# Five routing groups instead of six, a floor inside a scan, and a reordered passage between attention and mixture of experts

## The chip, the cores and the metric

The kernel runs on one core of a Trainium2 chip. Its time is device microseconds from launch to end; the median of three runs before the change is 373.67 us (373.53 to 373.78). The profile is of a separate execution, recorded by the hardware profiler. Engines are called PE (TensorE, matrix products; PEld is its weight load), DVE (VectorE), ACT (ScalarE), POOL (GpSimd) and SP (SyncE, which here only issues transfers). Each engine works through its own queue in order and waits on semaphores for the others.

## The reference

Attention with a decaying state, then a top-1 mixture of experts on its output, all in float32:

```python
for t in range(S):                       # B, H, S, D = 4, 8, 768, 48
    state = alpha[:, :, t, :, None] * state + einsum('bhd,bhe->bhde', k[:, :, t], v[:, :, t])
    y[:, :, t] = einsum('bhd,bhde->bhe', q[:, :, t], state)
x = y.transpose(0, 2, 1, 3).reshape(3072, 384)
logits = x @ w_gate + modality_bias[modality_id]       # 8 experts, 2 modalities
e_idx = argmax(logits); gate_w = softmax(logits)[e_idx]
for e in range(8):
    mask = e_idx == e
    out[mask] = gate_w[mask, None] * (relu(x[mask] @ w1[e]) @ w2[e])   # 384 -> 1024 -> 384
```

## The kernel before, in words

**Attention.** The 3072 tokens are 24 chunks of 128 tokens, one chunk per step, some 5.5 us each. In a step DVE makes the decay products of the chunk with two scans: `decay` scans backwards to G (L254), `decay_back` takes the column `amin` out of G with a floor (L262), its reciprocal (L263), and scans forwards to Fw (L265). G times the transposed keys is kh (L281), Fw times the transposed queries is qh (L289). PE transposes kh back (L295), multiplies qh with the state (L327) and with kh (L307), and after a causal select on POOL (L312) multiplies the scores with the values (L334). The state update is POOL's (L356, L358). The rows of the result, y, are transposed again (L365), multiplied with the gate weights (L377), and the products are turned into logits (L385, L387).

**Routing.** When the logits of a group of chunks are there, `route_flow` adds the bias table, finds the winning expert and each token's rank among that expert's tokens (L445 to L473: six DVE operations to `oh`, products with a triangle and with ones on PE, then ranks and the one-hot table `OL`). `GROUPS` says which chunks form a group and after which step it starts. Flows are generators: every step takes each of them one `yield` further, so the work of a flow is spread over steps. Two experts are begun early (`EARLY`): at the given chunk `route_early` picks an expert that already has 256 tokens, finds their places (products at L567), and `gather` fetches their rows (xg, POOL's indirect transfers, L689). After the second early expert `gates_flow` computes the gates of all tokens so far (gt, L673 to L675), PE transposes them (L678), ACT copies them (gs, L680), SP writes them to memory (gd, L685), and `gather_gates` fetches the early experts' gates (gg, POOL, L695).

**The passage.** Behind the last attention step stands a hand-written sequence in which `first_unit(0)` to `first_unit(7)` fill PE: each is three float32 products of the first layer of the first early expert (L124). Between them stand the last group, the count of each expert's tokens and the plan of slots (`route_end`, L592 to L621: nj, nn, ..., diag on DVE; key and meta), the tables of places (L636 to L648), and the gather for the third slot. `relu` makes hH and hL from a unit pair (ACT L823, DVE L825).

**Mixture of experts.** Every float32 operand of a product is split in a high and a low part: ACT casts the high part (w1H, w2H, hH), the low part is the difference (w1L, w2L by `split`, L833). A layer-2 product is the three products w2H·hH, w2L·hH and w2H·hL (L1001 to L1003). Four splits `split2(0, 0)` to `split2(0, 3)` prepare w2 of the first early expert; each serves two of the eight blocks of 128 hidden units.

**What sets the order.** On PE, DVE and ACT the order is the order of the code. The order on POOL and SP is set by a scheduler, so POOL's operations, its gathers among them, stand in one queue whose sequence the code alone doesn't show. Weights are loaded by SP in halves of 768 KB (w1r L661, w2r L663).

Of the kernel before, what the change touches and what calls it, by code (L numbers as in the profile page):

```python
# [8 lines left out]
F32 = mybir.dt.float32  # L9
# [5 lines left out]
ALU = mybir.AluOpType  # L15
# [6 lines left out]
P = 128  # L22
# [3 lines left out]
SEG = P + 1  # L26
# [15 lines left out]
U = T // P  # L42
NG = 2 * E

EARLY = (16, 18)
NA = len(EARLY)
NE = NA * TE // T
SU = N // T
# [7 lines left out]
AMIN = 1.0e-17  # L56
AFLOOR = 1.0e-30

GROUPS = ((5, 0, 6), (11, 6, 12), (15, 12, 16), (17, 16, 18), (21, 18, 22), (23, 22, 24))


@with_exitstack
def attention_moe(ctx: ExitStack, tc: tile.TileContext, q, k, v, alpha, mid, wg, mb, w1, w2, out):
# [13 lines left out]
    na = nctx.enter_context(tc.tile_pool(name="na", bufs=1, side="right"))  # L77
# [78 lines left out]
                wg.rearrange("(h c g d) e -> c g d h e", c=2, g=2, d=D)[c, g],  # L156
            )
    DR = na.tile([P, SEGS], F32, name="DR")[:, : NP * SEG + 1]
    vec.memset(DR, 0.0)
    vec.memset(DR[:, SEG :: SEG], 1.0)  # L160
    X, DF, T1 = [], [], []
    for i in range(2):
# [49 lines left out]
    def bias_table():  # L212
        mf = ac.tile([NU, P], F32, name="mf")
        vec.tensor_copy(mf, mi[:, :, 0])
        yield
        mp = ps.tile([P, NU], F32, name="sc", bufs=2)
        pe.transpose(mp, mf, ident[:NU, :NU])
        mt = ac.tile([P, NU], F32, name="mt")
        vec.tensor_copy(mt, mp)
        tmp = ac.tile([P, NU, E], F32, name="btt")  # L220
        for m in range(NM):
            sel = ac.tile([P, NU], F32, name=f"msel{m}")
            vec.tensor_scalar(sel, mt, float(m), None, op0=ALU.is_equal)
            vec.tensor_tensor(
                tmp if m else bt,
                sel.unsqueeze(2).broadcast_to([P, NU, E]),
                mbb[:, m].unsqueeze(1).broadcast_to([P, NU, E]),
                op=ALU.mult,
            )
            if m:  # L230
                vec.tensor_tensor(bt, bt, tmp, op=ALU.add)
# [19 lines left out]
    def decay(i):  # L251
        x = X[i % 2]
        G = na.tile([P, SEGS], F32, name="G", bufs=4)[:, : NP * SEG + 1]
        vec.tensor_tensor_scan(  # L254
            G[:, 1:][:, ::-1], x[:, 1:][:, ::-1], DR[:, 1:][:, ::-1], 0.0, op0=ALU.mult, op1=ALU.add
        )
        st[i, "G"] = G

    def decay_back(i):
        x, d, G = X[i % 2], DF[i % 2], st[i, "G"]  # L260
        ac1 = amin[:, i]
        vec.tensor_scalar(ac1, G[:, 1::SEG], AFLOOR, None, op0=ALU.max)  # L262
        vec.reciprocal(d[:, 0::SEG], ac1)  # L263
        Fw = na.tile([P, SEGS], F32, name="Fw", bufs=3)[:, : NP * SEG]
        vec.tensor_tensor_scan(Fw, x[:, :-1], d, 0.0, op0=ALU.mult, op1=ALU.add)  # L265
        st[i, "F"] = Fw
# [167 lines left out]
    def route_flow(t0, t1):  # L434
        n = t1 - t0
        s = slice(t0, t1)
        sh = [P, n, E]

        def wide(a, m=E):
            return a[:, s].unsqueeze(2).broadcast_to([P, n, m])  # L440

        def over(a, m=E):
            return a.unsqueeze(1).broadcast_to([P, n, m])

        vec.tensor_tensor(L[:, s], L[:, s], bt[:, s], op=ALU.add)  # L445
        vec.tensor_reduce(mx[:, s], L[:, s], axis=AX.X, op=ALU.max)
        vec.tensor_tensor(ls[:, s], L[:, s], wide(mx), op=ALU.subtract)
        vec.scalar_tensor_tensor(eq[:, s], ls[:, s], 0.0, over(rev), op0=ALU.is_equal, op1=ALU.mult)
        vec.tensor_reduce(m2[:, s], eq[:, s], axis=AX.X, op=ALU.max)
        vec.tensor_tensor(oh[:, s], eq[:, s], wide(m2), op=ALU.is_equal)  # L450
        yield
        rp = ps.tile([P, n, E], F32, name="sc", bufs=2)
        pe.matmul(rp, tri, oh[:, s], start=True, stop=False)
        for t in range(t0, t1 - 1):
            m = t1 - 1 - t
            pe.matmul(
                rp[:, t + 1 - t0 :], ones, oh[:, t].unsqueeze(1).broadcast_to([P, m, E]), start=False, stop=False
            )
        pe.matmul(rp, ones, ohs.unsqueeze(1).broadcast_to(sh), start=False, stop=True)
        vec.tensor_tensor(rk[:, s], rp, oh[:, s], op=ALU.mult)  # L460
        yield
        with nc.allow_low_precision("whole numbers"):
            vec.tensor_reduce(r1[:, s], rk[:, s], axis=AX.X, op=ALU.add)
        if t1 == NU and n > 2:
            vec.tensor_reduce(hsum, oh[:, t0 : t1 - 1].rearrange("p t e -> p e t"), axis=AX.X, op=ALU.add)
            vec.tensor_tensor(ohs, ohs, hsum, op=ALU.add)
        elif t1 < NU:
            vec.tensor_reduce(hsum, oh[:, s].rearrange("p t e -> p e t"), axis=AX.X, op=ALU.add)
            vec.tensor_tensor(ohs, ohs, hsum, op=ALU.add)
        vec.tensor_scalar(hr[:, s], r1[:, s], 7, None, op0=ALU.arith_shift_right)  # L470
        vec.tensor_scalar(lo[:, s], r1[:, s], P - 1, None, op0=ALU.bitwise_and)
        vec.scalar_tensor_tensor(hi[:, s], m2[:, s], -float(NU), hr[:, s], op0=ALU.mult, op1=ALU.add)
        vec.tensor_tensor(OL[:, s], over(ioh, P), wide(lo, P), op=ALU.is_equal)  # L473
# [113 lines left out]
    def route_end(na):  # L587
# [3 lines left out]
        cnt = ps.tile([P, E], F32, name="kv")  # L591
        pe.matmul(cnt, ones, ohs, start=True, stop=False)  # L592
        pe.matmul(cnt, ones, left, start=False, stop=False)
        if na:
            pe.matmul(cnt, ones, oh[:, NU - 2], start=False, stop=False)
        pe.matmul(cnt, ones, oh[:, NU - 1], start=False, stop=True)
        vec.tensor_tensor(
            nj.rearrange("p e u j -> p e (u j)"),
            cnt.unsqueeze(2).broadcast_to([P, E, 2 * NJ]),
# [69 lines left out]
    def gates_flow(t0, t1):  # L669
        z = slice(t0, t1)  # L670
        sh = [P, t1 - t0, E]
        act.activation(ls[:, z], ls[:, z], AF.Exp)
        vec.tensor_reduce(sm[:, z], ls[:, z], axis=AX.X, op=ALU.add)  # L673
        vec.tensor_scalar(sm[:, z], sm[:, z], 1e-9, None, op0=ALU.add)
        vec.reciprocal(gt[:, z], sm[:, z])  # L675
        yield
        gp = ps.tile([t1 - t0, P], F32, name="kv")
        pe.transpose(gp, gt[:, z], ident)  # L678
        gs = cp.tile([t1 - t0, P], F32, name=f"gs{t0}_{t1}")
        act.copy(gs, gp)  # L680
        m = min(max(MID // P, t0), t1)
        yield
        for a, b in ((t0, m), (m, t1)):
            if a < b:
                sp.dma_start(gd[row(a) : row(a) + (b - a) * P].rearrange("(t p) o -> t (p o)", p=P), gs[a - t0 : b - t0])  # L685
# [98 lines left out]
    def group_flow(t0, t1):  # L784
        yield from route_flow(t0, t1)
        if t1 in EARLY:
            e = EARLY.index(t1)
            yield from route_early(e)
            gather(e, early_cols(e), row(t1))
            if e == NA - 1:  # L790
                yield from gates_flow(0, t1)
                for e in range(NA):
                    gather_gates(e, early_cols(e), row(t1))
# [3 lines left out]
    def advance():  # L797
        for f in list(flows):
            if next(f, f) is f:
                flows.remove(f)  # L800
# [24 lines left out]
        vec.scalar_tensor_tensor(hL, hp, 0.0, hH.bitcast(F32), op0=ALU.max, op1=ALU.subtract)  # L825
        return hH, hL

    def split(name, src):
        p = hpool[name]
        hi = p.tile(list(src.shape), F32R, name=name + "H", bufs=4)  # L830
        act.copy(hi, src)  # L831
        lw = p.tile(list(src.shape), F32R, name=name + "L", bufs=4)
        vec.tensor_tensor(lw, src, hi.bitcast(F32), op=ALU.subtract)  # L833
        return hi, lw

    def split1(w, j):
        return split("w1", WR[w][0][:, :, 2 * P * j : 2 * P * (j + 1)])

    def split2(w, j):
        return split("w2", WR[w][1][:, 2 * j : 2 * j + 2])  # L840

    route_begin()
    mctx = ExitStack()
# [52 lines left out]
    hpool["h"] = rctx.enter_context(tc.tile_pool(name="hp", bufs=8, side="right"))  # L896
    w2s, hs = {0: []}, {0: []}

    advance()
    early = flows.pop()  # L900
    logits(L0 - 2)
    state(L0 - 1)
    scores(L0)
    outputs(L0 - 1)
    logits_rows(L0 - 2)
    group = route_flow(GROUPS[-1][1] - 4, GROUPS[-1][1])
    next(group)
# [5 lines left out]
    for _ in group:
        pass
    next(early)
    first_inputs()
    logits(L0)
    rows(L0)
    logits_rows(L0)
    last = route_flow(GROUPS[-1][1], NU)  # L920
    next(last)
    flag = out_of_range()
    next(flag)
    first_unit(0)
    next(last)
    ends = route_end(NE)
    next(ends)
    first_unit(1)
    next(early)
    first_unit(2)  # L930
    next(ends)
    hs[0].append(relu(hp0[0], [P, 2, TE]))
    for _ in last:
        pass
    first_unit(3)
    for _ in flag:
        pass
    next(ends)
    w2s[0].append(split2(0, 0))
    first_unit(4)  # L940
    first_unit(5)
    hs[0].append(relu(hp0[1], [P, 2, TE]))
    for _ in ends:
        pass
    gather(2, slot_cols(1))
    for _ in early:
        pass
    first_unit(6)
    w2s[0].append(split2(0, 1))
    hs[0].append(relu(hp0[2], [P, 2, TE]))  # L950
    first_unit(7)
    w2s[0].append(split2(0, 2))
    hs[0].append(relu(hp0[3], [P, 2, TE]))
    w2s[0].append(split2(0, 3))

    actx.close()
    ectx = ExitStack()
# [291 lines left out]
```

## Time and profile before

| | |
|---|---|
| median of 3 runs | 373.67 us |
| profiled execution | 376.24 us, span 374.5 us, mean granted clock 0.990 |
| PE busy | 358.7 us, 96% |
| DVE busy | 225.1 us, 60% |
| ACT busy | 188.8 us, 50% |
| POOL busy | 149.2 us, 40% |
| attention steps | about 5 to 146 us of the span |
| passage | about 146 to 164 us |
| mixture of experts | about 164 us to the end |

In a timeline row stand the start, the duration, the engine, the line, the operation with output and inputs, the tile and the number of instructions; in brackets, how long the engine idled before it and what it waited for. A wait row gives the total, the number of waits and the longest. A row of stretches gives for each engine the busy time, then the granted clock of TensorE as a share of full speed, the share of the transfer engines and GB/s.

### The profile page before, as it was taken

To read this page: it belongs to the slowest core of one execution; us is meant where nothing else is said; L and a number is where in the kernel's file an instruction comes from. 1 tells how busy PE (TensorE), PEld (TensorE's weight loads), DVE (VectorE), ACT (ScalarE), POOL (GpSimd) and SP (SyncE) were. 2 spreads that over 40 slices of the span, in tenths; PEclk is the share of its full clock that TensorE was granted. 3 is DMA by queue.
4 is the path that set the end of the run, shared out by engine and by line. 5 is a ranking of instruction groups with operands and counts; after the bars stand their busy time and mean duration, and the time that the engine had idled before them with its cause. 6 is when DMAs were issued, how large, how long until landed. Compare 5 with 4: busy or idle time off the path is not lost. (4 is left out here: it accounts for less than half of the span.)

```text
span 374.5 us, 9357 instructions
## 1 busy us (share of the span) xinstructions
PE 358.7 (96%) x3663; PEld 315.8 (84%) x3663; DVE 225.1 (60%) x458; ACT 188.8 (50%) x367; POOL 149.2 (40%) x212
## 2 busy tenths in 40 slices
PE   7899899999999898999999999999999999999992
PEld 3788788888888696779998898899889988978992
DVE  6888879788989977885845506531660456036400
ACT  2677676776767564436555425433551445164410
POOL 9745336425436445163146335412722371220031
PEclk9999999999999899999999999999999999999997
DMA  9999999999999996668756326431723373110011
GB/s 136 162 168 165 197 184 198 192 182 186 191 191 188 206 333 232 220 207 316 215 168 196 126 79 224 155 107 47 270 84 123 128 223 111 69 44 5 1 45 49
DMA packets 122730, 59.18 MB, mean 158 GB/s; under 512 B 102857, under 2 KB 114168, under 8 KB 122676
## 3 DMA queue, kind: packets, MB, share of 16 engines
q1 hardware_dynamic: 118196, 48.78, 58.7%
q0 software_dynamic: 4032, 9.68, 7.7%
q8 instruction: 31, 0.51, 0.6%
q14 instruction: 23, 0.19, 0.2%
q10 hardware_dynamic: 448, 0.01, 0.1%
HBM read 49.01 MB, written 9.50 MB: 156 GB/s over the span
## 5 line engine op out<-in xcount | busy, mean ns | idle before, releaser
L967 POOL DMA_INDIRECT out_dram<-os,odx x23 | 23.4, 1016 | 110.4 <-ACT os L1035 94.7
L312 POOL TENSOR_SCALAR_AFFINE_SELECT scT<-scT 128x512 f32<-128x512 f32 x48 | 38.8, 831 | 65.8 <-ACT scT L311 65.7
L1001 PE MATMUL sc<-w2H,hH 128*128 128x384 f32 x192 | 65.0, 339 | 0.0
L1002 PE MATMUL sc<-w2L,hH 128*128 128x384 f32 x192 | 64.5, 336 | 0.5 <-DVE w2L L833 0.3
L1003 PE MATMUL sc<-w2H,hL 128*128 128x384 f32 x192 | 64.2, 334 | 0.0
L833 DVE TENSOR_TENSOR w1L<-w1r,w1H 128x768 fp32r<-128x768 f32 x24 | 22.0, 955 | 64.4 <-ACT w1H L831 61.6
L1020 PE MATMUL tr<-xH,w1H 128*128 128x512 f32 (+1 forms) x144 | 53.8, 374 | 0.0
L1022 PE MATMUL tr<-xH,w1L 128*128 128x512 f32 (+1 forms) x144 | 53.5, 372 | 0.0
L1021 PE MATMUL tr<-xL,w1H 128*128 128x512 f32 (+1 forms) x144 | 53.5, 371 | 0.0
L825 DVE SCALAR_TENSOR_TENSOR hL<-tr,hH 128x512 fp32r<-128x512 f32 x47 | 32.3, 688 | 34.1 <-ACT hH L823 27.4
L823 ACT ACTIVATE hH<-tr 128x512 fp32r<-128x512 f32 x47 | 28.0, 598 | 48.1 <-PE tr L1022 21.9
L1035 ACT ACTIVATE os<-sc,gg 128x384 f32<-128x384 f32 x23 | 13.4, 582 | 64.8 <-PE sc L1003 38.1
L1002 PEld LDWEIGHTS sc<-w2L,hH 128*128 128x128 f32 x192 | 36.1, 188 | 1.5 <-DVE w2L L833 1.5
L1001 PEld LDWEIGHTS sc<-w2H,hH 128*128 128x128 f32 x192 | 36.0, 188 | 1.1 <-issue 1.0
L1003 PEld LDWEIGHTS sc<-w2H,hL 128*128 128x128 f32 x192 | 36.0, 188 | 0.0
L695 POOL DMA_INDIRECT gg<-gd,idx x25 | 25.8, 1032 | 23.0 <-issue 14.8
L311 ACT COPY scT<-sc 128x512 f32<-128x512 f32 x48 | 25.8, 589 | 13.0 <-PE sc L307 13.0
L689 POOL DMA_INDIRECT xg<-xd,idx x25 | 27.2, 1086 | 12.7 <-DVE vals L524 6.0
L265 DVE TENSOR_TENSOR_SCAN Fw<-X,DF 128x516 f32<-128x516 f32 x24 | 30.9, 1286 | 0.8
L1022 PEld LDWEIGHTS tr<-xH,w1L 128*128 128x128 f32 x144 | 27.1, 188 | 4.7
L1020 PEld LDWEIGHTS tr<-xH,w1H 128*128 128x128 f32 x144 | 27.1, 188 | 4.7
L1021 PEld LDWEIGHTS tr<-xL,w1H 128*128 128x128 f32 x144 | 27.1, 188 | 4.6
(246 smaller groups left out, 679.2 us busy)
## 6 DMA issues: line engine op xcount, KB each, us to landing
w1r<-in_moe_w_dram SPq DMA_DIRECT2D x16, 768.0 KB
w2r<-in_moe_w_dram SPq DMA_DIRECT2D x16, 768.0 KB
nat_a<-in_alpha_dram SPq DMA_DIRECT2D x24, 192.0 KB
nat_k<-in_k_dram SPq DMA_DIRECT2D x24, 192.0 KB
nat_q<-in_q_dram SPq DMA_DIRECT2D x24, 192.0 KB
vt<-in_v_dram SPq DMA_DIRECT2D x24, 192.0 KB
xd<-xs SPq DMA_DIRECT2D x24, 192.0 KB
xg<-xd,idx POOLq DMA_INDIRECT x25
```

The source lines that it names most:

```text
L265: vec.tensor_tensor_scan(Fw, x[:, :-1], d, 0.0, op0=ALU.mult, op1=ALU.add)
L311: act.copy(s, pp[g])
L312: pool.affine_select(s, s, [[0, NP], [1, P]], ALU.is_ge, 0.0, base=0, channel_multiplier=-1)
L689: pool.indirect_dma_start(xg[x][:, u], None, xd[0:rows], IOA(idx[:, c : c + 1], 0), bounds_check=rows - 1, oob_is_err=False)
L823: act.activation(hH, hp, AF.Relu)
L825: vec.scalar_tensor_tensor(hL, hp, 0.0, hH.bitcast(F32), op0=ALU.max, op1=ALU.subtract)
L1001: pe.matmul(op, hH[:, us] if f is None else hH[:, f, us], wH, start=first, stop=False)
L1002: pe.matmul(op, hH[:, us] if f is None else hH[:, f, us], wL, start=False, stop=False)
L1003: pe.matmul(op, hL[:, us] if f is None else hL[:, f, us], wH, start=False, stop=final)
L1020: pe.matmul(hp, wH[:, d, fs], XH[:, d, :n], start=(d == 0), stop=False)
L1021: pe.matmul(hp, wH[:, d, fs], XL[:, d, :n], start=False, stop=False)
L1022: pe.matmul(hp, wL[:, d, fs], XH[:, d, :n], start=False, stop=(d == ND - 1))
```

## The change

- `GROUPS`: the groups end at chunks 6, 12, 16, 20, 24 instead of 6, 12, 16, 18, 22, 24; the second early expert is chosen at chunk 20 instead of 18. The last group is four chunks instead of two; the count therefore sums four `oh` products.
- The backward scan takes the maximum with a floor instead of adding zero, and the separate floor on DVE is gone. The check for too small products still reads `amin`, which POOL now copies from G.
- The bias table is made in one piece per modality, with a `yield` ahead of each.
- The passage is written in another order, and the subtraction of `split2(0, 3)` goes to POOL.

```diff
-EARLY = (16, 18)
+EARLY = (16, 20)
-GROUPS = ((5, 0, 6), (11, 6, 12), (15, 12, 16), (17, 16, 18), (21, 18, 22), (23, 22, 24))
+GROUPS = ((5, 0, 6), (11, 6, 12), (15, 12, 16), (19, 16, 20), (23, 20, 24))
+T0 = GROUPS[-1][1]
...
-    vec.memset(DR, 0.0)
+    vec.memset(DR, AFLOOR)
...
         for m in range(NM):
+            yield
...
-            G[:, 1:][:, ::-1], x[:, 1:][:, ::-1], DR[:, 1:][:, ::-1], 0.0, op0=ALU.mult, op1=ALU.add
+            G[:, 1:][:, ::-1], x[:, 1:][:, ::-1], DR[:, 1:][:, ::-1], 0.0, op0=ALU.mult, op1=ALU.max
         )
+        pool.tensor_copy(amin[:, i], G[:, 1::SEG])
...
-        vec.tensor_scalar(ac1, G[:, 1::SEG], AFLOOR, None, op0=ALU.max)
-        vec.reciprocal(d[:, 0::SEG], ac1)
+        vec.reciprocal(d[:, 0::SEG], G[:, 1::SEG])
...
-        if na:
-            pe.matmul(cnt, ones, oh[:, NU - 2], start=False, stop=False)
-        pe.matmul(cnt, ones, oh[:, NU - 1], start=False, stop=True)
+        for t in range(T0 if na else NU - 1, NU):
+            pe.matmul(cnt, ones, oh[:, t], start=False, stop=(t == NU - 1))
...
             if e == NA - 1:
+                yield
                 yield from gates_flow(0, t1)
...
-    def split(name, src):
+    def split(name, src, by=vec):
...
-        vec.tensor_tensor(lw, src, hi.bitcast(F32), op=ALU.subtract)
+        by.tensor_tensor(lw, src, hi.bitcast(F32), op=ALU.subtract)
```

The new passage, whole, as it stands now (before it: units 0 to 3 around the last two-chunk group and the count, 4 and 5 behind the first split, 6 and 7 behind the early flow, and the gather ahead of unit 6):

```python
    (early,) = flows
    next(early)
    logits(L0 - 2)
    next(early)
    state(L0 - 1)
    scores(L0)
    outputs(L0 - 1)
    next(early)
    logits_rows(L0 - 2)
    first_inputs()
    next(early)
    state(L0)
    rows(L0 - 1)
    next(early)
    outputs(L0)
    first_unit(0)
    logits(L0)
    rows(L0)
    next(early)
    logits_rows(L0)
    last = route_flow(T0, NU)
    next(last)
    flag = out_of_range()
    next(flag)
    first_unit(1)
    first_unit(2)
    next(last)
    ends = route_end(NE)
    next(ends)
    first_unit(3)
    for _ in last:
        pass
    first_unit(4)
    hs[0].append(relu(hp0[0], [P, 2, TE]))
    next(ends)
    next(early)
    next(ends)
    first_unit(5)
    next(early)
    for _ in flag:
        pass
    w2s[0].append(split2(0, 0))
    first_unit(6)
    hs[0].append(relu(hp0[1], [P, 2, TE]))
    for _ in early:
        pass
    first_unit(7)
    hs[0].append(relu(hp0[2], [P, 2, TE]))
    w2s[0].append(split2(0, 1))
    for _ in ends:
        pass
    gather(2, slot_cols(1))
    hs[0].append(relu(hp0[3], [P, 2, TE]))
    w2s[0].append(split2(0, 2))
    w2s[0].append(split2(0, 3, pool))
```

How it moves the instructions is seen at three places. First DVE in step 21, from the places of the first early expert (OHE) to kh; before:

```order
L560 TENSOR_TENSOR OHE<-OHE,tok_205 128x32
L445 TENSOR_TENSOR L<-L,bt 128x16
L446 TENSOR_REDUCE mx<-L 128x2
L447 TENSOR_TENSOR ls<-L,mx 128x16
L448 SCALAR_TENSOR_TENSOR eq<-ls,rev 128x16
L449 TENSOR_REDUCE m_212<-eq 128x2
L450 TENSOR_TENSOR oh<-eq,m_212 128x16
L262 TENSOR_SCALAR amin<-G 128x4
L263 RECIPROCAL DF_167<-amin 128x4
L265 SCALAR_TENSOR_TENSOR Fw<-X_165,DF_167 128x516
L281 TENSOR_TENSOR kh<-tr,G 128x512
```

and now, where the first six operations of a group and `amin` are no longer between the two:

```order
L555 TENSOR_TENSOR OHE<-key_222,hi 128x32
L561 TENSOR_TENSOR OHE<-OHE,tok_205 128x32
L264 RECIPROCAL DF_167<-G 128x4
L266 SCALAR_TENSOR_TENSOR Fw<-X_165,DF_167 128x516
L282 TENSOR_TENSOR kh<-tr,G 128x512
```

The group of chunks 16 to 19 now stands in step 23. Second, DVE in the passage, around the gates gt of the early tokens; before, gt stood ahead of the last group and of the count (nj to diag):

```order
L578 SCALAR_TENSOR_TENSOR K_251<-taken,K_249 128x8 x2
L673 TENSOR_REDUCE sm<-ls 128x18
L674 TENSOR_SCALAR sm<-sm 128x18
L675 RECIPROCAL gt<-sm 128x18
L387 TENSOR_REDUCE L<-kv 128x16
L445 TENSOR_TENSOR L<-L,bt 128x16
```

and now behind the count, the ranks of the last group, a low part hL and the keys:

```order
L615 TENSOR_SCALAR diag<-ident,kc 128x52
L464 TENSOR_REDUCE r_227<-rk 128x4
L471 TENSOR_SCALAR hr<-r_227 128x4
L472 TENSOR_SCALAR lo<-r_227 128x4
L473 SCALAR_TENSOR_TENSOR hi<-m_212,hr 128x4
L474 TENSOR_TENSOR OL<-ioh,lo 128x512
L826 SCALAR_TENSOR_TENSOR hL<-tr,hH 128x512
L620 CAST key<-kv 128x48
L621 CAST meta<-kv 1x12
L673 TENSOR_REDUCE sm<-ls 128x20
L674 TENSOR_SCALAR sm<-sm 128x20
L675 RECIPROCAL gt<-sm 128x20
```

Third, POOL behind its last select of the attention (xg_120 belongs to the second early expert, gg_122 and gg_123 to the two early experts' gates, xg_121 to the third slot, out_dram is the scatter of finished rows); before:

```order
L312 AFFINE_SELECT scT<-scT 128x512 x2
L689 DMA xg_120<-xd,idx 128x384 x2
L695 DMA gg_122<-gd,idx 128x1 x2
L695 DMA gg_123<-gd,idx 128x1 x2
L689 DMA xg_121<-xd,idx 128x384 x4
L967 DMA out_dram<-os,odx 3072x384 x2
```

and now:

```order
L313 AFFINE_SELECT scT<-scT 128x512 x2
L689 DMA xg_120<-xd,idx 128x384 x2
L695 DMA gg_122<-gd,idx 128x1 x2
L695 DMA gg_123<-gd,idx 128x1 x2
L689 DMA xg_121<-xd,idx 128x384 x4
L834 TENSOR_TENSOR w2L<-w2r_116,w2H 128x768
L967 DMA out_dram<-os,odx 3072x384 x2
```

The subtraction of the fourth split stands behind both series of gathers and ahead of the first scatter.

More of the change, by code (lines that the diff above doesn't have):

```diff
@@ L260, in decay_back @@
         x, d, G = X[i % 2], DF[i % 2], st[i, "G"]
-        ac1 = amin[:, i]
-        vec.tensor_scalar(ac1, G[:, 1::SEG], AFLOOR, None, op0=ALU.max)
-        vec.reciprocal(d[:, 0::SEG], ac1)
+        vec.reciprocal(d[:, 0::SEG], G[:, 1::SEG])
         Fw = na.tile([P, SEGS], F32, name="Fw", bufs=3)[:, : NP * SEG]
@@ L463, in route_flow @@
             vec.tensor_reduce(r1[:, s], rk[:, s], axis=AX.X, op=ALU.add)
-        if t1 == NU and n > 2:
+        if t1 == NU and t0 < T0:
             vec.tensor_reduce(hsum, oh[:, t0 : t1 - 1].rearrange("p t e -> p e t"), axis=AX.X, op=ALU.add)
@@ L837, in split1, with split2 @@
         return split("w1", WR[w][0][:, :, 2 * P * j : 2 * P * (j + 1)])
-    def split2(w, j):
-        return split("w2", WR[w][1][:, 2 * j : 2 * j + 2])
+    def split2(w, j, by=vec):
+        return split("w2", WR[w][1][:, 2 * j : 2 * j + 2], by)
     route_begin()
@@ L897, in attention_moe @@
     w2s, hs = {0: []}, {0: []}
-    advance()
-    early = flows.pop()
+    (early,) = flows
+    next(early)
     logits(L0 - 2)
+    next(early)
     state(L0 - 1)
@@ L904, in attention_moe @@
     outputs(L0 - 1)
+    next(early)
     logits_rows(L0 - 2)
-    group = route_flow(GROUPS[-1][1] - 4, GROUPS[-1][1])
-    next(group)
+    first_inputs()
     next(early)
@@ L910, in attention_moe @@
     rows(L0 - 1)
-    next(group)
+    next(early)
     outputs(L0)
[L913 to L916, printed above, removed]
+    first_unit(0)
     logits(L0)
     rows(L0)
+    next(early)
     logits_rows(L0)
-    last = route_flow(GROUPS[-1][1], NU)
+    last = route_flow(T0, NU)
     next(last)
@@ L923, in attention_moe @@
     next(flag)
-    first_unit(0)
+    first_unit(1)
+    first_unit(2)
     next(last)
@@ L927, in attention_moe @@
     next(ends)
[L928 to L932, printed above, removed]
+    first_unit(3)
     for _ in last:
         pass
-    first_unit(3)
+    first_unit(4)
+    hs[0].append(relu(hp0[0], [P, 2, TE]))
+    next(ends)
+    next(early)
+    next(ends)
+    first_unit(5)
+    next(early)
     for _ in flag:
         pass
-    next(ends)
     w2s[0].append(split2(0, 0))
-    first_unit(4)
-    first_unit(5)
+    first_unit(6)
     hs[0].append(relu(hp0[1], [P, 2, TE]))
+    for _ in early:
+        pass
+    first_unit(7)
+    hs[0].append(relu(hp0[2], [P, 2, TE]))
+    w2s[0].append(split2(0, 1))
     for _ in ends:
@@ L945, in attention_moe @@
     gather(2, slot_cols(1))
[L946 to L951, printed above, removed]
+    hs[0].append(relu(hp0[3], [P, 2, TE]))
     w2s[0].append(split2(0, 2))
-    hs[0].append(relu(hp0[3], [P, 2, TE]))
-    w2s[0].append(split2(0, 3))
+    w2s[0].append(split2(0, 3, pool))
     actx.close()
```

## The prediction

> **What bounds the kernel now.** I read the page's busy shares first, then TensorE's waits, then the stretches around the longest wait.
>
> ```profile
> PE 358.7 (96%) x3663; PEld 315.8 (84%) x3663; DVE 225.1 (60%) x458; ACT 188.8 (50%) x367; POOL 149.2 (40%) x212
> ```
>
> PE is busy for 358.7 of 374.5 us. Its waits, with total, count and longest, name what a reordering can still win:
>
> ```profile
> PE tr L295 <- DVE kh L281: 3.0, 3, 1.6
> PE sc L307 <- DVE qh L289: 1.2, 1, 1.2
> PE kv L377 <- issue: 0.9, 1, 0.9
> PE sc L1002 <- DVE w2L L833: 0.3, 2, 0.2
> ```
>
> So there is about 4.2 us of waiting for DVE in the attention steps and almost nothing later. The longest wait has a tail, as PE's timeline and the stretches show (busy time of each engine, then the granted clock):
>
> ```profile
> 59.31 0.66 PE L295 MATMUL tr<-ident,kh 128*128 128x128 f32 x4
> 61.94 1.09 PE L334 MATMUL y<-scT,vt 128*64 128x128 f32 x16
> ...
> 128.21 1.11 PE L295 MATMUL tr<-ident,kh 128*128 128x128 f32 x4 [1.63 <-DVE kh L281]
> 132.39 1.09 PE L334 MATMUL y<-scT,vt 128*64 128x128 f32 x16
> ```
>
> ```profile
> 124.80:128.24 3.44, 1.81 (x32) 1.66 (x30) 3.23 (x10) 1.06 (x2) 1.10 (x2) 1.00 0.76 165
> 128.24:131.65 3.41, 3.41 (x40) 2.27 (x44) 3.27 (x17) 1.45 (x4) 2.21 (x2) 0.50 0.91 303
> ```
>
> After a stretch with PE busy for only 1.81 of 3.44 us, the clock was half for 3.41 us. From L295 to L334 that took 132.39 - 128.21 = 4.18 us, against 61.94 - 59.31 = 2.63 in a like step: 1.55 lost. The profiled execution took 376.24 us for its 374.5 us span, the runs 373.67 in the median; I work in differences on the trace and add them to 373.67. Places are named on the time axis of before, with the gains ahead of the passage taken off at the end.
>
> **Group 16 to 18, floor and bias table: 4.5 us won.** DVE in step 21:
>
> ```profile
> 124.09 0.65 DVE L445 TENSOR_TENSOR L<-L,bt 128x16 f32<-128x16 f32 x1
> 125.93 0.16 DVE L262 TENSOR_SCALAR amin<-G 128x4 f32<-128x4 f32 x1
> 127.49 0.67 DVE L281 TENSOR_TENSOR kh<-tr,G 128x512 f32<-128x512 f32 x1
> ```
>
> The six group operations, from 124.09 to amin at 125.93, leave this step (1.84 us), and so does amin's 0.2 (125.93 to 126.13). kh moves from 127.49 to 125.45. PE had come to it 1.63 before 128.21, so the wait goes, and its 1.55 of half clock with it: 3.18. The group now stands in step 23, in place of the counts' four small operations, and moves kh there by some 0.3 at most. The bias table in two pieces takes half of
>
> ```profile
> 37.08 0.18 DVE L223 TENSOR_SCALAR msel<-mt 128x24 f32<-128x24 f32 x1
> 38.17 0.36 DVE L231 TENSOR_TENSOR bt<-bt,btt 128x192 f32<-128x192 f32 x1
> ```
>
> (37.08 to 38.45 with the next scan's start: 1.37) out of one step; with amin's 0.2 that covers the second of the three kh waits, 0.94. At the start amin leaves the chains to the first qh and the second kh, twice about 0.2: 0.4. Sum 3.18 + 0.94 + 0.4 = 4.5, and 4.0 to 5.0 as bounds. All other amin instructions (22 of 24) win nothing: DVE waits for PE's transposes there. The scan with max instead of add is costed like the one with add; a dearer one would be hidden by that same waiting. POOL's new copies of G into amin, one per step, are work of 128x4 that waits for G alone, and POOL idles between steps; nothing.
>
> **The passage: gates come later.** In before, DVE had the early tokens' gates (gt, 18 columns) before the last count began (nj):
>
> ```profile
> 147.83 0.68 DVE L473 TENSOR_TENSOR OL<-ioh,lo 128x512 f16<-128x512 f16 x1
> 149.43 0.30 DVE L673 TENSOR_REDUCE sm<-ls 128x18 f32<-128x144 f32 x1 [0.49 <-ACT ls L672]
> 149.98 0.27 DVE L675 RECIPROCAL gt<-sm 128x18 f32<-128x18 f32 x1
> 153.04 0.25 DVE L597 TENSOR_TENSOR nj<-kv,thr 128x96 f32<-128x96 f32 x1
> 155.49 0.25 DVE L615 TENSOR_SCALAR diag<-ident,kc 128x52 bf16<-128x52 f32 x1
> 156.42 0.69 DVE L825 SCALAR_TENSOR_TENSOR hL<-tr,hH 128x512 fp32r<-128x512 f32 x1
> ```
>
> In the new order gt stands behind the whole count. My walk: twenty early-count products now wait for some twenty DVE operations of step 23 (0.6 to 1.0), unit 0 stands ahead of logits, and so the last logits' transposes come at 151.64 where they stood at 150.47. Units 1 and 2 (1.39 each, from the row below) stand before the group's products: 154.7. The count ends at 155.1; nj to diag takes 155.74 - 153.04 = 2.70: 157.9. Then come r to OL (four small operations and a 512-wide OL, whose row starts 0.6 before its successor: 1.1), hL (again 0.6), key and meta (0.3) and sm to gt (149.98 + 0.27 - 149.43 = 0.82): 2.8 in all, gt at 160.7.
>
> From gt to the gathers the path is a transpose on PE, a copy on ACT, gd by SP, then POOL:
>
> ```profile
> 154.02 0.27 PE L678 MATMUL kv<-ident,gt 128*18 128x128 f32 x1
> 154.13 1.46 PE L124 MATMUL y<-xf,w1r 128*128 128x256 f32 x6
> ...
> 163.86 0.43 PE L1001 MATMUL sc<-w2H,hH 128*128 128x384 f32 x1
> ...
> 168.46 0.44 PE L1002 MATMUL sc<-w2L,hH 128*128 128x384 f32 x1 [0.15 <-DVE w2L L833]
> ```
>
> ```profile
> 154.61 0.68 SPq L685 DMA_DIRECT2D gd<-gs  x2
> ...
> 181.78 0.33 SPq L685 DMA_DIRECT2D gd<-gs  x1
> ```
>
> ```profile
> 134.51 0.59 POOL L356 TENSOR_TENSOR S<-S,T 128x192 f32<-128x192 f32 x1
> 135.18 0.51 POOL L358 TENSOR_TENSOR T<-S,G 128x192 f32<-128x192 f32 x1
> ...
> 157.17 0.99 POOL L695 DMA_INDIRECT gg<-gd,idx  x1 [7.79 <-issue]
> 161.13 0.99 POOL L695 DMA_INDIRECT gg<-gd,idx  x1 [0.30 <-issue]
> 163.46 0.99 POOL L689 DMA_INDIRECT xg<-xd,idx  x1 [1.33 <-DVE vals L524]
> 168.12 1.16 POOL L689 DMA_INDIRECT xg<-xd,idx  x1 [0.30 <-issue]
> 186.09 1.04 POOL L695 DMA_INDIRECT gg<-gd,idx  x1 [8.23 <-DMA gd<-gs]
> ```
>
> Before: L678 at 154.02, first gg at 157.17, so 3.15 for the path. With L678 at 160.75 the first gg comes at 163.9. The later gd took 186.09 - 181.78 = 4.31 from issue to its reader instead of 157.17 - 154.61 = 2.56, 1.75 more: 165.7 then. SP now also issues half of a w1 load ahead of gd, so I take the middle, 164.8.
>
> **POOL's queue: the split behind eight gathers.** The fourth split of expert 0's w2 is POOL's now, and its place in POOL's order is behind four gg and four xg. Four gg and the gap behind them take 161.13 + 0.99 + 0.30 - 157.17 = 5.25. Four xg take 168.12 + 1.16 - 163.46 = 5.82, or 4.95 if they went like the four gg (161.13 + 0.99 - 157.17); 5.4, and 0.3 to the next. The subtraction itself, 128x768 with two float inputs, has no row on POOL; the nearest are L358 and L356, 0.51 and 0.59 for 128x192. Four times that is 2.04 to 2.36; the low bound is the select over 128x512 at 1.22 for two (0.61 each, times 1.5: 0.9), the high one four times L356's mean of 0.70, 2.8:
>
> ```profile
> L312 POOL TENSOR_SCALAR_AFFINE_SELECT scT<-scT 128x512 f32<-128x512 f32 x44 | 34.8, 812 | 64.0 <-ACT scT L311 64.0
> L356 POOL TENSOR_TENSOR S<-S,T 128x192 f32<-128x192 f32 x15 | 10.5, 699 | 0.3
> L358 POOL TENSOR_TENSOR T<-S,G 128x192 f32<-128x192 f32 x18 | 9.3, 516 | 1.2
> ```
>
> I take 2.06, four times L358's mean. So w2L lands at 164.8 + 5.25 + 5.4 + 0.3 + 2.06 = 177.8; bounds 163.9 + 5.25 + 4.95 + 0.3 + 0.9 = 175.3 and 165.7 + 5.25 + 5.82 + 0.3 + 2.8 = 179.9.
>
> The Trainium skill, GPSIMD Engine Reference, section 3.1 Elementwise, has tensor_tensor on fp32 1.96 times slower there than on VectorE and keeps VectorE as the place for elementwise work. By DVE's own 0.95 for this subtraction an estimate from that page is 1.86 us, and the sum would be 0.2 less; no row here shows this shape on POOL.
>
> When would PE want it? Its first layer-2 product stood at 163.86. In the new order PE waits about 1.2 for gt, and reaches layer 2 near 164.9; DVE's places and splits hold it some 0.5 more, so the product with the fourth w2L (168.46 in before) would come near 169.9. It waits 177.8 - 169.9 = 7.9 us. PE works in order, so everything behind that product waits too: the other products of that half, the next expert's transposes. Against before this product is late by 177.8 - 168.46 = 9.3 (6.8 to 11.4), and PE is full afterwards, so none of it is caught up.
>
> A stall of 8 us leaves whole stretches of 3.4 us empty. Since 1.81 of 3.44 was enough for half clock, I expect half clock through the end of the stall and one to two stretches after it. Work of 3.41 us at half clock loses about half of that, 1.7; the row of 1.55 says the same. I take 1.8, with 1.0 and 2.7 as bounds (a part of one stretch, a stretch and a half).
>
> **Sum.** 9.3 + 1.8 - 4.5 = +6.6 us; 373.67 + 6.6 = 380.3. The bounds together give 6.8 + 1.0 - 5.0 = +2.8, 376.5, and 11.4 + 2.7 - 4.0 = +10.1, 383.8.
>
> **Rivals.** *The split is in time (faster).* If gathers only hand over descriptors and POOL's rows overstate how long they hold the queue, or gd lands far sooner, w2L is there when PE comes. Then PE carries only its own shift, 169.9 - 168.46 = 1.4, and the gains: 373.67 + 1.4 - 4.5 = 370.6. Against it: every gather row of before starts about 0.30 after the last has ended, and gg rows wait for gd. It decides once w2L lands before 169.9, eight microseconds sooner than my sum. Chance 0.10.
>
> *Only the xg series is in the way.* If gd is ready early, the split still stands behind xg, whose indices come from tables that PE finishes at about 164.8 (DVE copies: 166.0). 166.0 + 5.4 + 0.3 + 2.06 = 173.8: 5.3 late, with 1.2 for the clock, less 4.5: +2.0, 375.7. For it: DVE may come to gt sooner than my walk. Against: gt's place is behind the count. Chance 0.10.
>
> *Late signals.* In before xg's indices waited 1.57 us on DVE for products that PE had ended at 160.77, and the same would put the last xg further back, besides a second half-clock stretch: 1.6 + 1.7 on top, 383.6. Chance 0.10.
>
> ```profile
> 163.00 0.18 DVE L523 TENSOR_SCALAR idx<-kv 128x24 int32<-128x24 f32 x1 [1.57 <-remote]
> ```
>
> *No change.* The late part (stall and clock) shrinks to the 4.5 won, w2L at about 171.9. That needs both gg and xg shorter by half; chance 0.04.
>
> **Chances and range.** Forecast 0.66, its likeliest time 380.3; the rivals as given. Within 0.2%, 0.75 us, is about what a measurement of this kernel can't tell from no change: 0.04. Faster 0.10, slower 0.86. The range reaches from the second rival to just over the third: 375.4 to 384.0.
>
> **What would show it.** In the changed kernel's profile: one PE wait of 6 to 10 us at L1002 for POOL's w2L (L834), and no kh wait over 0.5 after the first steps; POOL's row of L834 right behind the fourth xg, 0.9 to 2.8 long; gg's first row about 7 us after nj's chain has ended, released by gd; granted clock 0.5 just after the stall. I am wrong if L834 ends before PE's product comes, if POOL takes other work ahead of gg, or if the time is under 373.

## The result and the profile after

The changed kernel takes 382.75 us in the median (382.23 to 384.11) against 373.6 us of the kernel before: a ratio of 1.0261, 95% interval 1.0221 to 1.0301. Slower, as forecast, and inside the range (375.4 to 384.0), but 2.4 us above the point of 380.3. The profiled execution took 382.77 us with a span of 380.3; the one of before 376.24 with 374.5.

The page's busy shares after:

```profile
PE 358.6 (94%) x3666; PEld 317.0 (83%) x3666; DVE 218.5 (57%) x419; ACT 189.3 (50%) x367; POOL 154.4 (41%) x237
```

TensorE's waits after (total, count, longest):

```profile
PE sc L1002 <- POOL w2L L834: 9.3, 1, 9.3
PE sc L1002 <- DVE w2L L834: 1.3, 1, 1.3
...
PE kv L678 <- DVE gt L675: 1.0, 1, 1.0
PE sc L308 <- DVE qh L290: 0.8, 1, 0.8
```

PE does the same work, 358.6 us. The three waits for kh are gone from the list, and one wait of 9.3 us for POOL's w2L stands at its head. POOL's timeline shows what that wait is made of:

```profile
161.06 1.00 POOL L695 DMA_INDIRECT gg<-gd,idx  x1 [15.59 <-DMA gd<-gs]
162.36 1.32 POOL L695 DMA_INDIRECT gg<-gd,idx  x1 [0.30 <-issue]
163.99 1.00 POOL L695 DMA_INDIRECT gg<-gd,idx  x1 [0.30 <-issue]
165.29 1.12 POOL L695 DMA_INDIRECT gg<-gd,idx  x1 [0.30 <-issue]
166.72 0.99 POOL L689 DMA_INDIRECT xg<-xd,idx  x1 [0.30 <-issue]
168.01 1.00 POOL L689 DMA_INDIRECT xg<-xd,idx  x1 [0.31 <-issue]
169.32 1.00 POOL L689 DMA_INDIRECT xg<-xd,idx  x1 [0.30 <-issue]
170.62 1.00 POOL L689 DMA_INDIRECT xg<-xd,idx  x1 [0.30 <-issue]
171.65 1.81 POOL L834 TENSOR_TENSOR w2L<-w2r,w2H 128x768 fp32r<-128x768 f32 x1
```

POOL stands still for 15.59 us until gd has landed, sends eight gathers, and only then subtracts. PE's timeline at the same place:

```profile
159.08 0.42 PE L1001 MATMUL sc<-w2H,hH 128*128 128x384 f32 x1
...
162.86 0.44 PE L1002 MATMUL sc<-w2L,hH 128*128 128x384 f32 x1 [1.28 <-DVE w2L L834]
...
173.51 0.69 PE L1002 MATMUL sc<-w2L,hH 128*128 128x384 f32 x1 [9.32 <-POOL w2L L834]
174.00 0.52 PE L1003 MATMUL sc<-w2H,hL 128*128 128x384 f32 x1
```

Layer 2 begins at 159.08 where it began at 163.86: the change had won 4.8 us by then. The product with the fourth w2L then stands at 173.51 instead of 168.46. The stretches around it give busy times by engine, the granted clock, the transfer share and GB/s:

```profile
166.40:169.80 3.40, 0.00 (x0) 0.00 (x0) 0.00 (x0) 0.00 (x0) 2.48 (x4) 0.50 0.23 66
169.80:173.20 3.40, 0.00 (x0) 0.00 (x0) 0.00 (x0) 0.00 (x0) 3.07 (x3) 0.50 0.60 164
173.20:176.60 3.40, 3.09 (x10) 3.10 (x11) 0.00 (x0) 1.04 (x2) 0.42 (x2) 0.50 0.53 158
176.60:180.00 3.40, 3.40 (x15) 3.40 (x14) 0.96 (x1) 0.26 (x1) 0.86 (x1) 0.67 0.54 166
```

In the first two rows, 6.8 us, no engine but POOL works, and the clock is half from inside the stall until about 178.8. From 173.51 on products follow each other every 0.32 us instead of 0.17: 16.5 of them in 5.3 us, 2.4 us lost.

### The profile page after: what moved, and what is told of

Read it like the earlier page. It is cut to its first block, busy times and chain, and to the rows that moved or that the text cites. A ratio compares the mean times of both kernels' runs of the same rounds, so it can differ in the third digit from the quotient of the medians.

```text
span 380.3 us, 9337 instructions
## 1 busy us (share of the span) xinstructions
PE 358.6 (94%) x3666; PEld 317.0 (83%) x3666; DVE 218.5 (57%) x419; ACT 189.3 (50%) x367; POOL 154.4 (41%) x237
## 5 line engine op out<-in xcount | busy, mean ns | idle before, releaser
L1002 PE MATMUL sc<-w2L,hH 128*128 128x384 f32 x192 | 65.6, 342 | 10.6 <-POOL w2L L834 9.3
L1001 PE MATMUL sc<-w2H,hH 128*128 128x384 f32 x192 | 66.0, 344 | 0.0
L1003 PE MATMUL sc<-w2H,hL 128*128 128x384 f32 x192 | 65.2, 340 | 0.0
L1002 PEld LDWEIGHTS sc<-w2L,hH 128*128 128x128 f32 x192 | 36.9, 192 | 11.3 <-POOL w2L L834 9.6
L1001 PEld LDWEIGHTS sc<-w2H,hH 128*128 128x128 f32 x192 | 36.8, 192 | 1.1 <-issue 1.0
L1003 PEld LDWEIGHTS sc<-w2H,hL 128*128 128x128 f32 x192 | 36.9, 192 | 0.0
L266 DVE TENSOR_TENSOR_SCAN Fw<-X,DF 128x516 f32<-128x516 f32 x24 | 32.5, 1352 | 0.8
L256 DVE TENSOR_TENSOR_SCAN G<-X,DR 128x516 f32<-128x516 f32 x24 | 30.1, 1256 | 0.0
```

What stands on the lines that cost most here:

```text
L256: vec.tensor_tensor_scan(G[:, 1:][:, ::-1], x[:, 1:][:, ::-1], DR[:, 1:][:, ::-1], 0.0, op0=ALU.mult, op1=ALU.max)
L1001: pe.matmul(op, hH[:, us] if f is None else hH[:, f, us], wH, start=first, stop=False)
L1002: pe.matmul(op, hH[:, us] if f is None else hH[:, f, us], wL, start=False, stop=False)
L1003: pe.matmul(op, hL[:, us] if f is None else hL[:, f, us], wH, start=False, stop=final)
```

## The experiments

All ratios are to the kernel before, run on the same chip beside the kernel; its own median differed between the three groups of runs (375.45, 375.42 and 372.91 us), so only ratios are compared. Places in the traces shift too: the same attention code brings the first of four weight loads ahead of the passage to 141.44 in the changed kernel's profile and to between 141.09 and 143.58 in the runs that share that code. The theory: the fourth split waits in POOL's queue behind two series of gathers, the first of which the reordered passage has made late. Rivals: late gates or the reordered passage cost by themselves, or subtraction on POOL harms wherever it stands.

**The split back on DVE.** One line of the changed kernel:

```diff
-    w2s[0].append(split2(0, 3, pool))
+    w2s[0].append(split2(0, 3))
```

> The changed kernel with the fourth split's subtraction back on DVE, nothing else. Queue theory: DVE does it right behind the third split, ready before PE comes to it (its product stood at 164.19 when the wait began), so the 9.3 us wait and the 2.4 us of half clock behind it go: 382.75 - 11.7 = 371.0, below before's 373.6. The other DVE wait of 1.3 us stays. Rival, the late gates cost by themselves: the first os on ACT, which needs gg, holds PE's tiles, and 2 us or more remain: 373 or above.

Measured: ratio 0.9940 (0.9916 to 0.9965), median 373.47 beside 375.45. PE's waits:

```profile
PE sc L1002 <- DVE hL L826: 1.3, 1, 1.3
PE y L145 <- DVE still L140: 1.3, 1, 1.3
PE kv L678 <- DVE gt L675: 1.1, 1, 1.1
```

The first row is the old wait for the third w2L: it names hL, and that w2L is DVE's next operation. The 9.3 us are gone, the rest of the change stays, and the kernel is 0.6% faster than before. From 1.0261 to 0.9940 is 3.2%, 12 us, against 9.3 + 2.4 = 11.7 from the profile. The loss is in that line. The gates and gathers are as late here as in the changed kernel (first gg at 162.01), so late gates alone don't make the kernel slower.

**The changed kernel again, on the chip of the last group.** No edit.

> The changed kernel once more, beside the others on the same chip: theory and rival both expect the ratio of 1.026 again, with PE's wait of 9.3 us; it gives the loss that the runs with the split elsewhere are to be held against.

Measured: 1.0264 (1.0225 to 1.0303). The wait in its profile was 8.3 us: gg began 0.6 sooner (160.45) and the gathers ran a little shorter. The ratio is the same.

**Only the split on POOL, in the kernel before.**

```diff
-    w2s[0].append(split2(0, 3))
+    w2s[0].append(split2(0, 3, pool))
```

> The kernel before with only the fourth split's subtraction on POOL. Queue theory: before's xg series ended at 169.28, the subtraction takes 1.81, so w2L at 171.1 where PE wants it at 168.3: a wait of 2.8 us, and half clock behind it if that stretch of 3.4 us is mostly empty (up to 1.7): 376.4 to 378.1. Rival, the subtraction on POOL does no harm and the loss comes from the reordered passage: 373.6.

Measured: 1.0114 (1.0067 to 1.0160), 4.3 us. POOL's timeline, TensorE's waits and the stretches around the wait in this run:

```profile
168.16 0.99 POOL L689 DMA_INDIRECT xg<-xd,idx  x1 [0.30 <-issue]
169.17 1.82 POOL L833 TENSOR_TENSOR w2L<-w2r,w2H 128x768 fp32r<-128x768 f32 x1
```

```profile
PE sc L1002 <- POOL w2L L833: 2.7, 1, 2.7
```

```profile
169.80:173.20 3.40, 2.15 (x8) 2.16 (x9) 2.01 (x1) 0.45 (x1) 1.19 (x1) 0.75 0.84 268
173.20:176.60 3.40, 3.40 (x17) 3.40 (x16) 0.96 (x1) 0.85 (x2) 1.03 (x1) 0.75 0.85 258
```

The place in the queue does harm without any reordering: 2.7 us of waiting (2.8 expected), and half clock for one stretch (0.75 in two neighbouring rows) makes up the rest. In the old passage the gathers of gates are over by then, and only xg is in the way. The reordered passage turned 2.7 us into 9.3.

**The split on POOL, but ahead of the gathers.**

```diff
     first_unit(2)
+    fourth = split2(0, 3, pool)
     next(last)
...
-    w2s[0].append(split2(0, 3, pool))
+    w2s[0].append(fourth)
```

> The changed kernel with the fourth split made already behind unit 2: ACT casts it in an idle stretch, and POOL subtracts ahead of the gg gathers, while it idles. Queue theory: ready near 152, no wait, same as with the split on DVE: 371.0, perhaps 0.5 less since DVE is relieved. Rival, POOL's subtraction is harmful wherever it stands (it slows DVE or the gathers behind it): 372.5 or above.

Measured: 0.9973 (0.9947 to 1.0000). POOL subtracts at 149.78, in a stretch in which it idles, and PE has no wait for that w2L. POOL's row, and one of ACT's timeline further on:

```profile
149.78 1.83 POOL L834 TENSOR_TENSOR w2L<-w2r,w2H 128x768 fp32r<-128x768 f32 x1 [2.17 <-ACT w2H L832]
```

```profile
176.44 0.58 ACT L1036 ACTIVATE os<-sc,gg 128x384 f32<-128x384 f32 x1 [6.01 <-remote]
```

So it is the place in the queue and not the engine that made the 12 us. A small harm of the kind the rival means isn't excluded: the theory's 371.0 would be a ratio of 0.993, the rival's 372.5 one of 0.997, and the run came out at the rival's edge, some 0.3% above the split on DVE with overlapping intervals. In its profile ACT's second os begins 4 us after its last product, and PE then waits 2.0 us in four places, two of them for ACT's and DVE's w1 parts. That profile is of the slowest of the twelve executions (376.98), and whether the waits come from this order or from that execution was not tried.

**The gates early, POOL's order unchanged.**

```diff
     logits_rows(L0)
+    next(early)              # exp, sums, gt
     last = route_flow(T0, NU)
...
     first_unit(1)
+    next(early)              # transpose, gs
     first_unit(2)
+    for _ in early:          # gd, gathers of the gates
+        pass
...
     next(ends)
-    next(early)
     next(ends)
     first_unit(5)
-    next(early)
...
-    for _ in early:
-        pass
     first_unit(7)
```

> The changed kernel with the gates of the early tokens (exp, gt, transpose, gs, gd) taken ahead of the last group, the POOL order unchanged with the split behind all gathers. Queue theory: gg is done before 160, xg starts with its indices (159.9) and takes 5.2, w2L 1.8: 167.0 instead of 173.5. PE loses its 1.0 wait for gt and wants w2L near 163.2: a wait of 3.8 instead of 9.3. 382.75 - 1.0 - 5.5 = 376.3, 0.8 less if the half clock gets shorter. Rival, the wait is not set by the series of gathers: still above 381.

Measured: 1.0116 (1.0069 to 1.0164), where the expected times make 1.005 to 1.007: more than expected, at the edge of the interval. The wait shrank to 3.8 us, as expected; POOL's timeline and TensorE's waits:

```profile
158.19 1.18 POOL L695 DMA_INDIRECT gg<-gd,idx  x1 [10.79 <-DMA gd<-gs]
...
169.25 1.81 POOL L834 TENSOR_TENSOR w2L<-w2r,w2H 128x768 fp32r<-128x768 f32 x1
```

```profile
PE sc L1002 <- POOL w2L L834: 3.8, 1, 3.8
PE sc L1002 <- DVE hL L826: 2.5, 1, 2.5
```

That confirms the chain gates, gathers, w2L. It agrees by two errors that cancel, though. The series of gg began at 158.19, where it had to begin by about 154.7 to be over before 160, so that w2L was ready at 171.06 instead of 167.0. PE came to the fourth product at 167.4 instead of 163.2: this run's axis lies 1.9 us later (first load at 143.38), and PE's wait for the third w2L grew from 1.3 to 2.5 (the second row; it names hL, but the product starts when w2L, DVE's next operation, has ended). The odd part is gd, on SP's queue:

```profile
143.38 1.00 SPq L661 DMA_DIRECT2D w1r<-in_moe_w_dram  x2
144.56 1.15 SPq L663 DMA_DIRECT2D w2r<-in_moe_w_dram  x2
...
150.60 0.72 SPq L685 DMA_DIRECT2D gd<-gs  x2
```

A transfer of a few KB, issued at 150.60, let its reader start at 158.19, 7.6 us later; in the kernel before it took 2.56.

**gd through POOL's queue.** In the changed kernel:

```diff
-                sp.dma_start(gd[...], gs[...])
+                (pool if t0 == 0 else sp).dma_start(gd[...], gs[...])
```

> The changed kernel, the fourth split still on POOL behind the gathers, but the early gates' gd written through POOL's queue instead of SP's, where half of a w1 load stands ahead of it. Theory: gd landed 5.4 us after its issue because it ran behind that load's 768 KB; by POOL it lands in 2.5 to 3 us, the first gg comes near 158.5 instead of 161.1, and w2L about 2.5 us sooner: PE's wait 6.8 instead of 9.3, ratio to before 1.019 to 1.021. Rival, the landing time is not set by the load ahead: first gg again at 161, ratio 1.026.

Measured: 1.0241 (1.0192 to 1.0289); wait again 9.3. A miss. POOL's timeline:

```profile
158.20 1.14 POOL L685 DMA_DIRECT2D gd<-gs  x2 [10.66 <-ACT gs L680]
163.21 1.09 POOL L695 DMA_INDIRECT gg<-gd,idx  x1 [3.87 <-DMA gd<-gs]
```

It went out alone in another queue and still took 5.0 us to its reader. Counted from the first weight load, the first gg came as late as in the changed kernel: 163.21 - 143.52 = 19.7 here, 161.06 - 141.44 = 19.6 there. So the place behind the half w1 load in SP's queue is not what makes gd late. The load itself isn't excluded: SP issues it at 157.29 here, still ahead of gd.

**gd between the loads.** As with the gates early, but transpose, gs and gd stand behind unit 3:

```diff
     logits_rows(L0)
+    next(early)
     last = route_flow(T0, NU)
...
     first_unit(3)
+    next(early)
+    for _ in early:
+        pass
```

> The changed kernel, split still on POOL behind the gathers, with the early gates taken early but their transpose behind unit 3, so that gd is issued near 153, about 8 us after the last weight loads of before the passage and ahead of the next one. If gd's landing time of 5 to 7 us is the time of the loads that are still under way when it is issued, it lands here in about 2.6 us as in the kernel before, the first gg comes near 156.5, xg starts with its indices near 162 and PE's wait is 4 to 5 us: ratio 1.010 to 1.013. If the time has another cause, gg stays at 158 or later.

Measured: 1.0163 (1.0126 to 1.0200), above the expected 1.010 to 1.013, with a wait of 6.7 us instead of 4 to 5. gd was issued at 151.82 and its reader began at 156.78, 5.0 us later, not 2.6: the second miss on gd. The longer wait has a second reason: the four gg took 7.2 us here (xg began at 163.97), against 5.25 in the kernel before, because single gathers held the queue for up to 1.81 us. Laid side by side, the runs tell more. SP issues four weight loads of 768 KB ahead of the passage (first at 141 to 143); the reader of gd began

| run | first load | gd issued | first gg | gd issue to gg | first load to gg |
|---|---|---|---|---|---|
| kernel before | 142.69 | 154.61 | 157.17 | 2.6 | 14.5 |
| gd between the loads | 141.88 | 151.82 | 156.78 | 5.0 | 14.9 |
| gates early, split on POOL | 143.38 | 150.60 | 158.19 | 7.6 | 14.8 |
| third split first (below) | 143.42 | 150.63 | 158.63 | 8.0 | 15.2 |
| both splits first (below) | 141.09 | 148.31 | 155.82 | 7.5 | 14.7 |

Wherever gd was issued between 148 and 155, its reader began 14.5 to 15.2 us after the first of those loads (14.5, 14.8 and 15.7 in three runs that are not in the table). The stretches show why this looks like waiting for the loads: with the loads and the rows of xd and xg the transfer engines are full, at some 375 GB/s, until 153.2 to 155.6 in these five runs (the last stretch of 0.2 us with a share over 0.5), and gd's reader begins 2.2 to 3.0 us after that. In the kernel before gd was issued just as that stretch ended, and took 2.6 us. The changed kernel and the run with POOL's queue fit as well, with the half w1 load in place of the four: the stretches behind gd's issue differ in the transfer share, next to last, in the kernel before,

```profile
156.00:158.00 2.00, 2.00 (x10) 1.70 (x11) 1.82 (x10) 0.49 (x2) 0.83 (x1) 1.00 0.06 12
```

in the changed kernel,

```profile
157.00:159.00 2.00, 2.00 (x34) 1.80 (x33) 2.00 (x4) 1.97 (x4) 0.00 (x0) 1.00 0.93 347
```

and in the run with POOL's queue:

```profile
159.00:161.00 2.00, 2.00 (x33) 1.75 (x32) 2.00 (x5) 1.97 (x5) 0.35 (x1) 1.00 0.99 367
```

In the last two the engines were full until about 158.9 and 161.2, and the readers began 2.2 and 2.0 us later (1.5 to 1.6 in the three other runs with such a load beside gd). So in these runs gd's landing followed the end of the large transfers, whichever queue it was in. This was found afterwards; no run took the load beside gd away, so the cause is argued and not shown.

**Floor and bias table alone, in the kernel before.** The diff's parts for DR, both scans, amin and the `yield` in the bias table; groups, passage and splits of before.

> The kernel before with only the floor inside the scan (POOL copying amin) and the bias table in two pieces; its groups, its passage and its splits stay. Theory: PE's wait of 0.94 for kh (bias table) goes and those for the first qh and the second kh get shorter by 0.2 each; the 1.63 in step 21 gets shorter by 0.2 only, since the group of chunks 16 and 17 stays there: -1.3 to -1.5 us, ratio 0.996. Rival, POOL's copies or the max in the scan cost something in each of 24 steps: no gain or a loss.

Measured: 0.9983 (0.9956 to 1.0009): not told apart from no change, and the expected 0.996 is inside the interval too. TensorE's waits:

```profile
PE tr L295 <- DVE kh L281: 1.4, 1, 1.4
PE sc L1002 <- DVE w2L L833: 1.3, 1, 1.3
```

The wait of 0.94 is gone, the first qh's wait went from 1.2 to 0.5, and the wait in step 21 stayed, as expected: PE stood 1.2 us earlier in the passage (the tables' products at 158.78, before 160.01). There part of it was given back, in a new wait of 1.3 for the second w2L. DVE has the places' indices ahead of that w2L, and it idled for them:

```profile
162.91 0.18 DVE L523 TENSOR_SCALAR idx<-kv 128x24 int32<-128x24 f32 x1 [2.66 <-PE y L989]
```

The products that it needs had ended near 159.5 on PE. In the kernel before they ended at 160.8, and DVE went on at 163.00: at the same time in both, about a microsecond after POOL's gg series (last row 160.97 + 1.00 here, 161.13 + 0.99 before).

**Gates early and the fourth split on DVE.** The gates' edit above together with the first edit.

> The run with the early tokens' gates ahead of the last group, and the fourth split on DVE as well. Theory: against the changed kernel with the split on DVE only the 1.0 us wait of PE for gt goes, and the 1.3 to 2.5 us wait for the third w2L (held back on DVE by the places' indices) stays or grows: ratio to before 0.990 to 0.994. Rival, the gathers of the gates matter to the output side: clearly below 0.990.

Measured: 0.9936 (0.9908 to 0.9964), in the expected band and no better than with late gates: the 1.0 for gt goes, and the wait for the third w2L grows from 1.3 to 2.5:

```profile
PE sc L1002 <- DVE w2L L834: 2.5, 1, 2.5
```

With the gates early, gg again runs while the tables' products end, and DVE again idles for them (1.11 us here).

**The third split ahead of the places' indices.** On top of the last run:

```diff
     w2s[0].append(split2(0, 1))
+    w2s[0].append(split2(0, 2))
     for _ in ends:
         pass
     gather(2, slot_cols(1))
     hs[0].append(relu(hp0[3], [P, 2, TE]))
-    w2s[0].append(split2(0, 2))
```

> The same with the third split also moved ahead of the places' indices on DVE. Theory: PE's wait for the third w2L (1.3 to 2.5 us) goes too, nothing else moves since the indices' gathers stand behind gg: ratio to before 0.985 to 0.989. Rival, later indices hold up xg and the next slot's transposes: a PE wait for xg appears and the ratio stays at 0.991 or more.

Measured: 0.9917 (0.9891 to 0.9943), not the 0.985 to 0.989 of the theory; it is the rival's figure without the rival's wait, for TensorE's list has no wait for xg. The intervals of this run and the last overlap. The wait moved on, to 1.1 us for the fourth w2L.

**Both splits ahead of the indices.** On top of that, `relu` of the last pair and `split2(0, 3)` go ahead of the indices too.

> The run with gates early, the fourth split on DVE and the third split ahead of the places' indices, with the fourth split moved ahead of them too. Theory: PE's last wait of 1.1 us for a w2L goes, and the indices come 1.5 us later, which the gg series still covers: ratio to before 0.988 to 0.990. Rival, the later indices or the later meta hold up the next slot: a new PE wait for xg or a weight, ratio 0.992 or more.

Measured: 0.9929 (0.9903 to 0.9955), 369.74 beside 372.91 us. The expected 0.988 to 0.990 lies just below the interval, though the waits did go; 0.9929 is the rival's figure, but the wait for xg or a weight that it needs isn't there. TensorE's list of waits begins with

```profile
PE y L145 <- DVE still L140: 1.3, 1, 1.3
PE sc L308 <- DVE qh L290: 1.1, 1, 1.1
PE y L989 <- DVE hL L826: 0.5, 1, 0.5
PE sc L568 <- DVE OHE L561: 0.5, 1, 0.5
```

The first two lie at the start; behind it nothing over 0.5 us is left. The four versions with the fourth split on DVE (0.9917 to 0.9940) can't be told apart by their intervals; each is faster than both kernels of this case.

## Why the prediction was right, step by step

Times of the prediction stand on the axis of before; on the changed kernel's own axis they are 4.5 less.

| step | predicted | measured |
|---|---|---|
| waits for kh, floor, table (without half clock) | 4.5 - 1.55 = 3.0 | kh waits 3.0 to 0, first qh 1.2 to 0.8 |
| early-count products | wait 0.6 to 1.0 | 0.45 |
| gt ready | 160.7 - 4.5 = 156.2 | 154.91 |
| first gg | 160.3 | 161.06 |
| four gg | 5.25 | 5.66 |
| four xg and gap | 5.7 | 4.93 |
| subtraction on POOL | 2.06 | 1.81 |
| w2L ready | 173.3 | 173.46 |
| PE wants it | 165.4 | 164.2 |
| stall | 7.9 | 9.3 |
| half clock | 1.8 | 2.4 |

The mechanism and its place held, as both the split on DVE and the split early on POOL show. Three sizes were off. gt came 1.3 us sooner than my walk had it; 0.9 of that stood already at the last logits' transposes (146.25 instead of 151.64 - 4.5 = 147.1), a step for which the prediction gives no terms. Yet from gt to the first gg took 6.15 us, where I had 3.2 to 5.0: gd's landing, bounded by 2.56 and 4.31, took 5.4. With the four xg 0.8 shorter, these nearly cancelled: that w2L ended within 0.2 us of the forecast is partly luck. PE, too, came 1.2 us sooner, and so waited longer; that lengthens the stall, not the end. One of the signs that the prediction names came out otherwise: gg's first row stood 8.8 us behind the end of nj's chain (152.29), not about 7.

The subtraction took 1.81 us. The nearest rows, times four, had given 2.06; the estimate from the Trainium skill (GPSIMD Engine Reference, section 3.1 Elementwise: 1.96 times VectorE's time) was 1.86, and this trace agrees with it: 1.81 / 0.95 = 1.9.

Against its own basis the sum was good: from profiled execution to profiled execution the change cost 382.77 - 376.24 = 6.5 us, forecast 6.6. That closeness, too, is partly luck: PE's last product came 7.0 us later (374.07, before 367.08), and the span behind that product, which lay between 5.7 and 7.5 us in the thirteen profiles of this case, happened to be 1.2 us shorter. Against the medians the change cost 9.15. **The term that was mis-sized is one of the gains**: I credited the change with 1.55 us of half clock behind the wait in step 21 and added the difference to a median. The profiled execution of before was 2.6 us slower than its median, and its half-clock stretch is not in every execution of this code. The run with only the split on POOL has the same wait at the same place, as its PE timeline and stretches show:

```profile
128.53 0.66 PE L295 MATMUL tr<-ident,kh 128*128 128x128 f32 x4 [1.63 <-DVE kh L281]
```

```profile
124.80:128.20 3.40, 2.09 (x34) 1.94 (x32) 3.16 (x10) 1.19 (x3) 1.35 (x3) 1.00 0.67 152
128.20:131.60 3.40, 2.86 (x59) 2.03 (x59) 3.26 (x16) 1.45 (x4) 1.88 (x2) 1.00 1.02 380
```

Full clock throughout (1.00), where before's profile had 0.50; the run of floor and bias table, with 1.43, was at 1.00 too. And over the 59 executions of the kernel before beside the experiments the mean granted clock lay between 0.985 and 0.999, in 49 of them above the 0.990 of that profile. How many of the executions behind the median have the half clock in step 21 isn't shown, so the size of this error is argued. Without the 1.55 the forecast would have been 6.6 + 1.55 = 8.2 and 381.8. The 0.6 by which the half clock behind the stall was too small makes 8.8. The rest, 0.4, has a place that the prediction left out: outside the core's span the four runs of the changed kernel took 1.9 to 2.5 us (2.4 in the median), the 59 of the kernel before 1.7 to 1.9. What makes it longer was not tried.

The Trainium skill (TensorE: Matmul & The Clock Gate, What's actually happening) describes a free-running activity window of 3413 ns and half clock after an idle one. The 3.41 us stretch agrees with the length, and one wait that halves the clock in one execution and not in another fits a window that doesn't start with the kernel. But in before's profile the stretch ahead was busy for 1.81 of 3.44 us, so a half-filled one was enough there.

Of the rivals, the split in time and the one with xg alone in the way fell: gg did stand ahead. The late signals did not show on the way to w2L: DVE had xg's indices by 160.0, long before gg ended. They showed in some other runs, where gg ran while the tables' products ended (last section).

## What to carry to other kernels

Work put on an engine that "has time" joins that engine's queue: read what stands ahead of it there and what that waits for, not the engine's busy share (POOL was 41% busy and cost 12 us). Moving a producer later (here the gates) cost nothing that could be measured (0.9940 late, 0.9936 early) until something else stood behind its consumer. When a forecast is made from one profiled execution, compare that execution with the median first, and count nothing that depends on where a clock window happened to fall.

## What was not expected of the hardware

- A transfer of a few KB took 2.6 to 8.0 us to its reader. In the five runs of the table its reader began 2.2 to 3.0 us after the transfer engines had last been full, whenever it was issued before; issuing it from another engine's queue, beside a load, didn't help (5.0 us).
- Two runs with the same 1.63 us wait of TensorE at the same place had half clock for 3.41 us behind it in one and full clock in the other.
- In runs in which POOL's gg series ran while PE ended the tables' products, DVE got to the indices late: it idled 1.57 us in the kernel before, 2.66 with floor and bias table, 1.11 with the gates early; in the changed kernel, where gg came later, it did not idle. With gd between the loads gg ran at that time as well, and DVE had the products within 1.8 us of their end without idling. What holds the signal up isn't shown.
- An indirect gather mostly held POOL's queue for 1.3 us (1.0 and a gap of 0.30), whether it moved one word or 384 per row: 0.99 is the shortest for gg and for xg. Single ones held it longer, up to 2.13 for xg with the gates early and the split on DVE, and 2.63 for gg with the third split first. In eight profiles with 64 gathers, each one over 1.2 us overlapped by 0.4 us or more with a DVE subtraction of 128x768 or an xL; none that overlapped by less than 0.3 us took longer than 1.2. No run tried this.
